# Where in its 256 bytes a stationary operand starts: AT_G from 56 to 16 elements

## The chip, the core and the metric

The kernel runs on one core of a Trainium2 chip. The metric is device time in microseconds (us), the median of several executions. The engines are TensorE (PE in the profile; its loads of stationary operands are listed as PEld), VectorE (DVE), ScalarE (ACT), GpSimd (POOL) and SyncE (SP), whose queue issues the transfers.

## What is computed

An attention over packed tokens feeds a two-layer network with silu. All arrays are float32.

```
p_packed = softmax(p k^T / 8) v             # 8 batches x 8 heads, 32 packed tokens from 576
x        = softmax(q p_packed^T / 8) p_packed   # then heads side by side: 4608 rows x 512
h        = x @ w_in                          # 512 -> 2048
g        = h * sigmoid(h)
out      = g @ w_out                         # 2048 -> 512
```

## The kernel before

Every large product is made of three products of halves. An operand is split into an upper part (a copy rounded to float32r, names that end in `_hi`) and a lower part (the operand less that copy, names that end in `_lo`), and upper by upper, upper by lower and lower by upper are added up in PSUM. In `nc.tensor.matmul(out, a, b)` the operand `a` is the stationary one: a weight load (LDWEIGHTS) puts its 128 columns into TensorE, and then the columns of `b` stream past.

The order of the work is written out by hand in `ORDER`, a text of steps, each a letter and a unit number, and the engines take the steps in that order. The first two batches run while the weights are still being made (up to about 195 us). After that come batches 2 to 7. A **pair unit** (there are 96: six batches, two halves of the rows, eight pairs of hidden blocks) covers 256 rows and two blocks of 128 hidden columns, and its output product is done with Strassen's scheme in seven products instead of eight. Its steps are

- `B`: `h_products` (L590), 12 matmuls with 288 moving columns; its stationary operands are `pw_hi` and `pw_lo`.
- `G` and `N`: `pair_values` (L612) and `rest_values` (L616), the silu on ScalarE. L612 writes the first four blocks of the tile `g`, eight blocks of 128 columns.
- `I`: `pair_sums` (L622 to L624) on GpSimd, four more blocks of `g` as sums and differences.
- `F`: `all_upper` (L638) on ScalarE, the upper part of seven of these blocks, 896 columns, into a tile `g_hi`.
- `L`: `all_lower` (L642) on VectorE, the lower part, into `g_lo`.
- `O`: `pair_products` with `terms` (L648), seven terms of three matmuls. The stationary operand is a block of 128 columns of `g_hi` or `g_lo`; the moving one is 256 columns of `wo_hi`, `wo_lo` or of `sums_of_w`, loaded from DRAM.

The tiles `g_hi` and `g_lo` come from the pool `gp_main`, two of each. They are 7 x 128 + 64 = 960 columns wide, so that the 896 columns of a pair unit may start anywhere in the first 64: `all_upper` starts them at `AT_G`. A row of a tile is 3840 bytes, 15 times 256, and in the built program every one of these tiles starts at a multiple of 256 bytes, as do the tiles of `wo_hi`, `wo_lo`, `sums_of_w`, `pw_hi`, `pw_lo` and `rest`. A block of 128 columns is 512 bytes, so all seven blocks of a unit start equally far past a multiple of 256.

A **rest unit** (16 of them: four for batches 0 and 1 together, twelve for batches 2 to 7) is the same for the 32 rows of each half that the pairs leave: 512 columns of `g_hi` and `g_lo` that start at 0, twelve matmuls of 512 moving columns, on the same lines L638, L642 and L648. The output product of the first two batches (also on L648, with `g_hi` and `g_lo` made at L602 and L608) has 512 moving columns and starts at 0 too.

Of the kernel before, what the change touches and what calls it, by code (L numbers as in the profile page):

```python
# [121 lines left out]

TP_BUFS = 4
EDGE = 504
AT_G = 56
ON_TOKENS = (0,)
SCALE = 1.0 / math.sqrt(D)
EPS = 1e-9
# [5 lines left out]
def packed_attention_ffn(ctx: ExitStack, tc: tile.TileContext, pkT, qT, v, w_in, w_out, out):  # L134
# [491 lines left out]
    def all_of(u):  # L626
        b, f, *more = units[u]
        if more:
            return rest[:, f : f + FJ].rearrange("p f e h s -> p (f e h s)")
        return hidden[u][:, P:]  # L630

    def all_upper(u):
        g = all_of(u)
        at = AT_G if g.shape[1] > FJ * P else 0
        both = [gp_main.tile([P, 7 * P + 64], F32R, name=name) for name in ("g_hi", "g_lo")]
# [284 lines left out]
```

## Time and profile before

| | |
|---|---|
| median of 3 executions | 694.07 us (693.35 to 694.8) |
| the profiled execution's own time | 693.81 us |
| its span | 692.0 us, granted TensorE clock 0.995 |
| busy: PE, PEld, DVE, ACT, POOL | 672.5, 591.5, 425.8, 387.0, 233.6 us |
| share of the chain that ended last: PE, DVE, ACT, DMA | 76%, 10%, 5%, 3% |

The span runs from the first to the last instruction that the profiler recorded; the profiled execution's own time holds 1.8 us outside it. Busy time counts the time in which at least one instruction of an engine was under way. A matmul's recorded duration holds its run through the array, so that matmuls in a row overlap; the distance of their starts, not the duration, says how fast they follow each other.

### The profile page before, as it was taken

Reading aid. Unit: us, or ns where it says so; the run is one execution under the profiler, and the core shown is the slowest. Engines: PE = TensorE matmul, PEld = TensorE weight load, DVE = VectorE, ACT = ScalarE, POOL = GpSimd, SP = SyncE. Lnnn points to the kernel's source line nnn. Section 1 sums busy time; section 2 is a strip of 40 time slices with the busy share of each in tenths; the row PEclk is TensorE's granted clock in tenths of the full one; section 3 lists DMA queues with packets and bytes.
Section 4 is the critical chain, followed back from the end, with each engine's and each line's share of the span. In section 5 each row is a group of like instructions: output and inputs, shape, how many; then the busy total and the mean of one; then the engine's idle time right before and its main releaser. Section 6 shows DMA issues by size and latency. Waiting matters only on the chain.

```text
span 692.0 us, 14725 instructions
## 1 busy us (share of the span) xinstructions
PE 672.5 (97%) x5958; PEld 591.5 (85%) x5958; DVE 425.8 (62%) x588; ACT 387.0 (56%) x641; POOL 233.6 (34%) x336
## 2 busy tenths in 40 slices
PE   7799999999999999999999999999999999999997
PEld 5477776788878998999888998899888898899995
DVE  5989989896774536753666425853665535663333
ACT  5787887463645535663556634755554754664431
POOL 1102054343203432544423343353251353435520
PEclk9899999999999999999999999999999999999999
DMA  9848864685967678967797578874994848685531
GB/s 362 328 136 307 282 222 173 235 267 184 386 242 283 247 245 329 363 251 262 283 342 282 184 284 308 348 279 131 353 353 168 303 132 307 265 313 190 212 139 45
DMA packets 55107, 178.62 MB, mean 258 GB/s; under 512 B 21760, under 2 KB 25856, under 8 KB 47360
## 3 DMA queue, kind: packets, MB, share of 16 engines
q1 hardware_dynamic: 54944, 177.56, 69.1%
q8 instruction: 47, 0.77, 0.4%
q10 hardware_dynamic: 96, 0.13, 0.1%
q14 instruction: 20, 0.16, 0.1%
HBM read 149.42 MB, written 24.12 MB: 251 GB/s over the span
## 4 chain that ended last, share of the span: by engine, by line
PE 76%; DVE 10%; ACT 5%; DMA 3%; issue 2%; POOL 2%; SPq 1%; ACTq 0%; DVEq 0%
PE ps_acc L648 45%; PE ps_two L590 23%; PE ps_two L287 5%; DMA win<-in_w_out 2%; PE ps_two L387 2%; DVE tm L423 1%; DVE g_lo L642 1%; DMA sums_of_w<-sums_of_w 1%; DVE g_lo L608 1%; DVE w_raw L252 1%; ACT g_hi L638 1%; DVE w_raw L256 1%; ACT g L612 1%; DVE wo_lo L280 1%; POOL g L623 1%
## 5 line engine op out<-in xcount | busy, mean ns | idle before, releaser
L642 DVE TENSOR_TENSOR g_lo<-g,g_hi 128x896 fp32r<-128x896 f32 x96 | 105.9, 1110 | 131.6 <-ACT g_hi L638 131.2
L648 PE MATMUL ps_acc<-wo_hi,g_hi 128*128 128x256 f32 (+1 forms) x576 | 184.7, 321 | 0.7 <-DVE o L790 0.7
L648 PE MATMUL ps_acc<-wo_hi,g_lo 128*128 128x256 f32 (+1 forms) x576 | 183.0, 318 | 2.2 <-DVE g_lo L608 2.2
L648 PE MATMUL ps_acc<-wo_lo,g_hi 128*128 128x256 f32 (+1 forms) x576 | 182.7, 317 | 0.0
L590 PE MATMUL ps_two<-a_hi,pw_hi 128*128 128x288 f32 x512 | 153.0, 299 | 1.5 <-DVE tm L423 1.5
L622 POOL TENSOR_TENSOR g<-g 128x128 f32<-128x128 f32 x96 | 56.2, 586 | 288.0 <-ACT g L612 287.9
L590 PE MATMUL ps_two<-a_lo,pw_hi 128*128 128x288 f32 x512 | 151.3, 295 | 0.0
L590 PE MATMUL ps_two<-a_hi,pw_lo 128*128 128x288 f32 x512 | 151.1, 295 | 0.0
L638 ACT CAST g_hi<-g 128x896 fp32r<-128x896 f32 x96 | 89.9, 942 | 77.6 <-POOL g L624 47.5
L648 PEld LDWEIGHTS ps_acc<-wo_hi,g_hi 128*128 128x128 f32 x576 | 108.1, 188 | 16.1 <-issue 5.6
L648 PEld LDWEIGHTS ps_acc<-wo_hi,g_lo 128*128 128x128 f32 x576 | 108.2, 188 | 12.4 <-DVE g_lo L608 4.7
L648 PE MATMUL ps_acc<-sums_of_w,g_hi 128*128 128x256 f32 x576 | 116.6, 284 | 0.0
L648 PEld LDWEIGHTS ps_acc<-wo_lo,g_hi 128*128 128x128 f32 x576 | 108.3, 188 | 6.8 <-DVE wo_lo L280 0.3
L590 PEld LDWEIGHTS ps_two<-a_hi,pw_hi 128*128 128x128 f32 x512 | 96.5, 188 | 14.4 <-PE ps_two L287 6.7
L590 PEld LDWEIGHTS ps_two<-a_lo,pw_hi 128*128 128x128 f32 x512 | 96.4, 188 | 0.8
L590 PEld LDWEIGHTS ps_two<-a_hi,pw_lo 128*128 128x128 f32 x512 | 96.5, 188 | 0.0
L648 PEld LDWEIGHTS ps_acc<-sums_of_w,g_hi 128*128 128x128 f32 x576 | 88.3, 188 | 8.9 <-issue 7.8
L648 PE MATMUL ps_acc<-sums_of_w,g_lo 128*128 128x256 f32 x288 | 80.5, 280 | 0.1
L623 POOL TENSOR_TENSOR g<-g 128x256 f32<-128x256 f32 x96 | 75.5, 787 | 6.6
L612 ACT ACTIVATE g<-ps_two 128x512 f32<-128x512 f32 x96 | 57.0, 598 | 33.4 <-DVE g_lo L642 16.8
L624 POOL TENSOR_TENSOR g<-g 128x128 f32<-128x128 f32 x96 | 53.2, 556 | 6.6
L648 PEld LDWEIGHTS ps_acc<-sums_of_w,g_lo 128*128 128x128 f32 x288 | 54.1, 188 | 0.4 <-DVE g_lo L642 0.3
(129 smaller groups left out, 799.7 us busy)
## 6 DMA issues: line engine op xcount, KB each, us to landing
sums_of_w<-sums_of_w SPq DMA_DIRECT2D x96, 768.0 KB, 6.2
w_quarter<-w_in SPq DMA_DIRECT2D x22, 1024.0 KB, 6.9
kvq_t<-in_v SPq DMA_DIRECT2D x8, 1280.0 KB, 8.8
kvq_t<-in_pkT SPq DMA_DIRECT2D x7, 1216.0 KB, 10.7
out<-o SPq DMA_DIRECT2D x16, 512.0 KB, 3.2
kvq_t<-in_qT SPq DMA_DIRECT2D x7, 1152.0 KB, 8.3
w_raw<-in_w_in SPq DMA_DIRECT2D x6, 1024.0 KB, 6.1
sums_of_w<-w_sums SPq DMA_DIRECT2D x8, 768.0 KB, 3.7
```

The costliest lines, as they stand in the source:

```text
L252: nc.vector.tensor_scalar(up.bitcast(F32), up.bitcast(F32), TOP, -TOP, op0=ALU.min, op1=ALU.max)
L256: nc.vector.scalar_tensor_tensor(low, up, -(2**31), low, op0=ALU.bitwise_and, op1=ALU.bitwise_or)
L287: nc.tensor.matmul(bank(par)[NP * i : NP * i + NP], lhs(r, i), rhs(r, i), start=True, stop=True)
L387: nc.tensor.matmul(self.ps[NP * i : NP * i + NP, par * D : par * D + D], e, vs[:n, c, h * D : h * D + D], start=(c == 0), stop=(c == 4),)
L590: nc.tensor.matmul(bank, p[:, par, cols], a[:, par], start=(n == 0), stop=(n == len(todo) - 1))
L612: nc.scalar.activation(g[:, : 4 * P].rearrange("p (e s) -> p e s", e=2), made["h", u, None][..., :MAIN], AF.Silu)
L622: nc.gpsimd.tensor_tensor(x[:, 4], x[:, 0], x[:, 2], ALU.subtract)
L623: nc.gpsimd.tensor_tensor(x[:, 5:7], x[:, 0:5:4], one, ALU.subtract)
L624: nc.gpsimd.tensor_tensor(x[:, 7], x[:, 3], x[:, 6], ALU.add)
L638: nc.scalar.copy(both[0], g)
L642: nc.vector.tensor_tensor(g_lo, g, g_hi.bitcast(F32), ALU.subtract)
L648: nc.tensor.matmul(out, g[:, rows], w, start=(first and n == 0), stop=(last and n == 2), skip_group_check=True)
```

## The change

`AT_G` is a number of float32 columns. At 56 the 896 columns of a pair unit's `g_hi` and `g_lo` start 224 bytes into their tiles, at 16 they start 64 bytes in. Nothing else differs: the tiles are as large and lie where they lay, and on every engine the same instructions stand in the same order.

```diff
--- before.py
+++ after.py
@@ -122,7 +122,7 @@
 
 TP_BUFS = 4
 EDGE = 504
-AT_G = 56
+AT_G = 16
 ON_TOKENS = (0,)
 SCALE = 1.0 / math.sqrt(D)
 EPS = 1e-9
```

## Rows read from the trace of the kernel before

**Rows 1.** Busy time of each engine by stretch; (x) counts instructions; PEclk is the granted clock.

```profile
core 0: us, PE busy (x) PEld busy (x) DVE busy (x) ACT busy (x) POOL busy (x), PEclk, DMA share, GB/s
...
215.00:370.00 155.00, 154.32 (x1487) 142.02 (x1486) 87.60 (x122) 83.93 (x138) 60.21 (x95) 1.00 0.77 284
370.00:520.00 150.00, 149.18 (x1448) 136.03 (x1447) 84.14 (x112) 83.29 (x135) 59.15 (x95) 1.00 0.75 281
520.00:676.00 156.00, 155.51 (x1349) 146.61 (x1348) 75.13 (x100) 79.46 (x133) 61.77 (x96) 1.00 0.61 224
```

**Rows 2.** Chain that ended last, 215 to 676 us, share by engine and line.

```profile
by line: PE ps_acc L648 51.2%; PE ps_two L590 28.3%; PE ps_two L287 5.3%; PE ps_two L387 1.8%; DVE tm L423 1.5%; issue 1.5%; DVE g_lo L642 1.4%; DMA sums_of_w<-sums_of_w 1.3%; ACT g_hi L638 1.0%; ACT g L612 0.9%; POOL g L623 0.8%; POOL g L6
```

**Rows 3.** Chain, 290 to 352 us, in order of time: start us, us, what.

```profile
298.32 0.95 ACT g_hi L638
299.29 1.18 DVE g_lo L642
...
311.51 0.95 ACT g_hi L638
...
340.65 2.01 DVE g_lo L642 x2
...
348.60 1.10 DVE g_lo L642
```

**Rows 4.** What TensorE itself waited for, 195 to 676 us: total us, times, longest.

```profile
PE ps_two L590 <- DVE tm L423: 1.2, 5, 0.2
PE ps_two L287 <- DVE tm L423: 0.5, 2, 0.2
```

**Rows 5.** Instructions on tiles `g_hi`: count, ns min/median/max, first and last start.

```profile
L648 PEld LDWEIGHTS ps_acc<-wo_lo,g_hi x576: 186/188/192, 38.1 to 687.2; 128*128 128x128 f32 x192
...
L648 PEld LDWEIGHTS ps_acc<-sums_of_w,g_hi x576: 186/188/192, 220.3 to 675.2; 128*128 128x128 f32 x192
...
L638 ACT CAST g_hi<-g x96: 925/943/968, 215.0 to 671.2; 128x896 fp32r<-128x896 f32 x96
L642 DVE TENSOR_TENSOR g_lo<-g,g_hi x96: 1027/1092/1465, 216.0 to 672.2; 128x896 fp32r<-128x896 f32 x96
...
L638 ACT CAST g_hi<-rest x16: 602/622/631, 196.3 to 682.4; 128x512 fp32r<-128x512 f32 x16
L642 DVE TENSOR_TENSOR g_lo<-rest,g_hi x16: 628/692/1233, 199.8 to 683.1; 128x512 fp32r<-128x512 f32 x16
```

**Rows 6.** All groups of instructions, shapes apart: L739 and L743, the sums of the weights.

```profile
L743 DVE TENSOR_TENSOR w_sums<-w_pair,w_sums 128x1024 fp32r<-128x1024 f32 x8 | 9.8, 1219 | 4.8 <-ACT w_sums L739 4.8
...
L739 ACT CAST w_sums<-w_pair 128x1024 fp32r<-128x1024 f32 x8 | 8.4, 1055 | 10.4 <-POOL w_pair L734 7.8 <-DMA first_sums<-w_sums 2.5
```

**Rows 7.** All groups of instructions, shapes apart: matmuls of L648 by operands and moving columns.

```profile
L648 PE MATMUL ps_acc<-sums_of_w,g_hi 128*128 128x256 f32 x576 | 116.6, 284 | 0.0
...
L648 PE MATMUL ps_acc<-wo_hi,g_hi 128*128 128x256 f32 x384 | 107.7, 281 | 0.0
L648 PE MATMUL ps_acc<-wo_lo,g_hi 128*128 128x256 f32 x384 | 107.5, 280 | 0.0
L648 PE MATMUL ps_acc<-wo_hi,g_lo 128*128 128x256 f32 x384 | 107.2, 279 | 0.0
...
L648 PE MATMUL ps_acc<-sums_of_w,g_lo 128*128 128x256 f32 x288 | 80.5, 280 | 0.1
```

**Rows 8.** Chain, 360 to 412 us, columns as in rows 3.

```profile
362.98 3.19 PE ps_two L590 x24
366.17 8.22 PE ps_acc L648 x36
...
382.40 3.20 PE ps_two L590 x24
385.60 4.95 PE ps_acc L648 x42
...
399.02 4.96 PE ps_acc L648 x42
```

**Rows 9.** Chain, 518 to 542 us, same columns.

```profile
520.77 4.96 PE ps_acc L648 x42
...
532.88 8.17 PE ps_acc L648 x36
```

## The prediction

> **What bounds the kernel now.** I read the time by stretches first. From 215 to 676 us, where all 96 pair units run, TensorE is busy in 154.32 + 149.18 + 155.51 = 459.0 of 461 us at a granted clock of 1.00, the full 2.4 GHz, while no other engine is busy much over half of the time [rows 1]. Then the chain of that stretch: its pieces on TensorE come to 51.2 + 28.3 + 5.3 + 1.8 = 86.6%, half of it on L648 alone, the line that reads the moved operands [rows 2]. The rest is short runs of ScalarE, VectorE and GpSimd such as [rows 3], in which the chain goes through the making of `g_hi` and `g_lo`. TensorE's own waits say how much slack is behind them: 1.7 us in all [rows 4]. So in this stretch time is the number of matmuls times the distance of their starts, and little could swallow a longer distance.
>
> **The change part by part.** No instruction is added, removed or moved, no transfer changes. What changes is the start address of three kinds of operation, by 224 - 64 = 160 bytes: the write of L638 on ScalarE, the second input and the output of L642 on VectorE, and the weight load of every matmul of a pair unit. I price each.
>
> *ScalarE and VectorE.* The same two lines run with operands at start 0 (the rest units, 512 columns) and at 224 (the pair units, 896). L638 takes 622 and 943 ns, L642 692 and 1092 ns [rows 5]. Both lines have a like at start 0 with 1024 columns, in the sums of the weights: L739 takes 1055 ns and L743 1219 ns [rows 6]. Between 512 and 1024 columns, all at start 0, ScalarE then needs (1055 - 622) / 512 = 0.846 ns a column and VectorE (1219 - 692) / 512 = 1.029, which gives 947 and 1087 ns for 896 columns; at 224 they are 943 and 1092. I see no sign of an address cost on these engines and put 0 for both. The bounds: 20 ns either way on each of 96 units of either line is 1.9 us of an engine's time, and it would count only where the chain runs through them, 1.0% and 1.4% of the stretch [rows 2], so under 0.1 us. TensorE's other work is the cover.
>
> *TensorE.* The pair units have 576 + 3 x 384 + 288 = 2016 matmuls of 256 moving columns [rows 7], 96 x 21. How closely do they follow each other? The chain lists unbroken runs: 42 of them take 4.95 or 4.96 us, 117.9 ns each [rows 8, 9]. With the stationary operand at start 0 the trace has two other lengths: 288 columns, 24 in 3.19 or 3.20 us, 133.1 ns each [rows 8], and 512 columns, 36 in 8.17 to 8.22 us, 226.9 to 228.3 ns [rows 8, 9]. A straight line through these two has (226.9 - 133.1) / 224 = 0.419 ns a column, and gives 133.1 - 32 x 0.419 = 119.7 ns for 256 columns (119.5 with 228.3). The pair units run at 117.9, some 1.6 to 1.8 ns less. So either the fixed part of a matmul is not the same for each length, or a stationary operand that starts 224 bytes in is changed over faster than one that starts at 0. The weight load's own record is no help: 186 to 192 ns in groups with both starts [rows 5].
>
> Counted against 256 columns at 2.4 GHz, 106.7 ns, the pair units pay 11.2 ns beside the columns; 288 columns (120.0 ns) pay 13.1 and 512 (213.3 ns) pay 13.6. By this the start at 0 is dearer by 1.9 to 2.4 ns.
>
> No row shows a start of 64. The ends are then: nothing (64 is as good as 224), and the dearest reading of a start at 0, 2.4 ns x 2016 = 4.8 us. Of the two starts that the trace shows, 64 is nearer to 0 than to 224, by 64 against 96 bytes when one goes round at 256. I take a straight line from 0 to 224, so that 64 keeps 160/224 = 0.71 of the penalty of 0: 0.71 x 1.6 ns = 1.14 ns, and times 2016 it is 2.3 us. On the path counts between the chain's 0.87 and all of it, 2.0 to 2.3 us; I take 2.1. The profiled execution, 693.81 us, becomes 695.9; the median of the runs shown is 0.26 us above it, so the forecast is 694.07 + 2.1 = **696.2 us**.
>
> *A rule against it.* The rows show a difference that fits the start address but could come from the number of columns [rows 8, 9]. The Trainium skill, TensorE: Matmul & The Clock Gate, section Part 2: What happens when you issue a matmul, says that TensorE reads the streaming and the stationary operand through two independent SBUF ports, so that loading the next weights takes nothing from the running matmul; and SBUF — State Buffer, section Specifications (TRN2), gives lines of 16 bytes, of which both 224 and 64 are multiples. By these the start makes no difference and the sum is 694.1 us. No run here shows which holds.
>
> **The rivals.**
> - *It does nothing that a clock can see (same).* The 1.6 ns belong to the number of columns and not to the start, or 64 is as far from trouble as 224 is. For it: the two lengths at start 0 do not lie on one line with 2.4 GHz exactly either (13.1 and 13.6 ns), so half a nanosecond depends on length anyway; ScalarE and VectorE show nothing. Time: 694.1, within 0.2%, which is about what a measurement of this kernel can tell from no change, 1.4 us or 0.7 ns a matmul.
> - *The full penalty of start 0 (slower, more).* If the changeover knows only "at or near the beginning of 256 bytes" and "near its end", 64 counts as the beginning. Time: 1.6 to 2.4 ns x 2016 = 3.2 to 4.8 us, so 697.3 to 698.9.
> - *64 is better than 224 (faster).* The fixed part is still 11.2 ns, so there is something left to win; if what matters is how far the stationary reads lag behind or lead the moving ones, which all begin at a multiple of 256, a lead of 64 may miss them better than 224, which is 32 short of the next multiple. It decides from 0.7 ns a matmul on; as large as the difference of 0 and 224 it would give 694.1 - 3.2 = 690.9. Nothing in the rows speaks for it beyond that the direction is unknown.
> - *VectorE's subtraction suffers.* L642 reaches 1465 ns in one of its 96 [rows 5]; were every one so slow, 96 x 0.37 = 36 us of VectorE, a little of it on the chain (1.4% x a third = 2 us, 696). But the starts on record agree, and I give it no chance of its own.
>
> **How the numbers follow.** Forecast (a part of the penalty, over 0.7 ns a matmul): 0.39. Full penalty: 0.12. Nothing: 0.37. Better: 0.12. So slower by over 0.2%: 0.51; within: 0.37; faster: 0.12. The forecast and the case of nothing are close; the differing fixed parts of a matmul tip it. The range for 8 in 10 leaves out most of the faster case and the dearest tail: from 693.0 (the case of nothing, with the scatter of the runs shown below it) to 699.0 (the full penalty by its dearest count). The forecast's own range is 695.5 to 697.3.
>
> **What would show it.** Right: in the chain after, unbroken runs of 42 matmuls on L648 take 4.98 to 5.03 us in place of 4.95 (118.6 to 119.7 ns each), while 24 of L590 stay at 3.2 us and 36 of the rest units at 8.2 us; L638 and L642 keep 943 and 1092 ns; and the span grows by about 2016 times the growth of that distance. Same: the 42 stay at 4.95 or 4.96. Wrong in the other direction: 4.92 or less. Wrong in kind: the 42 stay, and yet the span moves, with VectorE's or ScalarE's median moved, or with new waits of TensorE; or the 42 grow and the span doesn't, so that slack I did not see took it up.

## The result and the profile after

The changed kernel takes 687.55 us (median of 4 executions, 687.07 to 688.15) against 694.04 for the kernel before (4 executions); the ratio is 0.9907 with a 95% interval of 0.989 to 0.9924. It is faster by 6.5 us, where 2.1 us slower was forecast. The profiled execution took 688.15 us, its span is 686.4 us (692.0 before) at a granted clock of 0.994.

The stages of the changed kernel, columns as in [rows 1], the last one 5 us shorter since the pair units end earlier:

```profile
215.00:370.00 155.00, 153.93 (x1494) 141.24 (x1493) 89.13 (x124) 83.53 (x139) 61.44 (x96) 1.00 0.78 288
370.00:520.00 150.00, 149.03 (x1468) 136.16 (x1467) 84.53 (x115) 83.79 (x136) 58.12 (x93) 1.00 0.74 277
520.00:671.00 151.00, 149.91 (x1322) 140.97 (x1320) 73.36 (x97) 79.44 (x132) 61.45 (x96) 1.00 0.62 231
```

TensorE is as busy as before at the same clock; it gets through the same matmuls sooner. Where, the chain of the changed kernel shows (355 to 412 us, start us, us, what; the view of [rows 8]):

```profile
356.28 4.96 PE ps_acc L648 x42
361.24 3.19 PE ps_two L590 x24
364.44 8.19 PE ps_acc L648 x36
...
375.23 5.42 PE ps_acc L648 x33
380.65 3.19 PE ps_two L590 x24
383.84 4.78 PE ps_acc L648 x42
388.62 1.02 PE ps_two L287 x16
389.64 1.79 PE ps_two L590 x12
391.43 2.48 PE ps_acc L648 x21
393.91 3.19 PE ps_two L590 x24
397.10 4.78 PE ps_acc L648 x42
```

The reader is to see two things. L590 (24 in 3.19 us) and the rest unit's 36 matmuls of 512 columns (8.19 us) are as before. Of the pair units, the runs of 42 at 383.84 and 397.10 us, both behind L590, take 4.78 us, 113.8 ns a matmul, where runs of 42 behind L590 took 4.95 or 4.96 before [rows 8, 9]; but the 21 at 391.43 us still take 2.48 us, 118.1 ns each. (The 42 at 356.28 us begin behind other work; both its units run at 113.3 once they have begun.) So there are two spacings, not one smaller one. TensorE's own lines show them, first a fast unit, then a slow one (the changed kernel's timeline, start us, us, engine, line; a row with x2 holds two matmuls):

```profile
386.08 0.39 PE L648 MATMUL ps_acc<-sums_of_w,g_hi 128*128 128x256 f32 x2
386.31 0.28 PE L648 MATMUL ps_acc<-sums_of_w,g_lo 128*128 128x256 f32 x1
386.42 0.28 PE L648 MATMUL ps_acc<-wo_hi,g_hi 128*128 128x256 f32 x1
386.53 0.28 PE L648 MATMUL ps_acc<-wo_lo,g_hi 128*128 128x256 f32 x1
386.65 0.28 PE L648 MATMUL ps_acc<-wo_hi,g_lo 128*128 128x256 f32 x1
386.76 0.28 PE L648 MATMUL ps_acc<-wo_hi,g_hi 128*128 128x256 f32 x1
```

```profile
391.27 0.40 PE L648 MATMUL ps_acc<-sums_of_w,g_hi 128*128 128x256 f32 x2
391.51 0.28 PE L648 MATMUL ps_acc<-sums_of_w,g_lo 128*128 128x256 f32 x1
391.62 0.28 PE L648 MATMUL ps_acc<-wo_hi,g_hi 128*128 128x256 f32 x1
391.74 0.28 PE L648 MATMUL ps_acc<-wo_lo,g_hi 128*128 128x256 f32 x1
391.86 0.28 PE L648 MATMUL ps_acc<-wo_hi,g_lo 128*128 128x256 f32 x1
391.98 0.28 PE L648 MATMUL ps_acc<-wo_hi,g_hi 128*128 128x256 f32 x1
```

From the first row's start to the last one's are six matmuls: 0.68 us in the fast unit, 0.71 in the slow one (all the starts of the two units in the trace lie 113 to 114 and 117 to 119 ns apart). Taken from the starts of all matmuls in the trace, unit by unit and without gaps over 150 ns, the mean spacing over the 96 units is 117.8 ns before and 114.6 after. Before, every unit lies between 116.6 and 118.1; after, 17 units lie at 117.6 to 117.9 and the other 79 at 113.3 to 114.8 (distances of 113 and 114 ns, with a few longer ones where a unit begins). 3.1 ns x 2016 is 6.3 us, the change of the medians is 6.5.

ScalarE and VectorE did not move (instructions on `g_hi` in the changed kernel, the view of [rows 5]):

```profile
L638 ACT CAST g_hi<-g x96: 923/942/967, 214.8 to 665.8; 128x896 fp32r<-128x896 f32 x96
L642 DVE TENSOR_TENSOR g_lo<-g,g_hi x96: 1028/1092/1445, 215.7 to 666.8; 128x896 fp32r<-128x896 f32 x96
```

### The profile page after: what moved, and what is told of

It is laid out like the page before. It is cut to its first block, busy times and chain, and to the rows that moved or that the text cites. A ratio compares the mean times of both kernels' runs of the same rounds, so it can differ in the third digit from the quotient of the medians.

```text
span 686.4 us, 14725 instructions
## 1 busy us (share of the span) xinstructions
PE 666.2 (97%) x5958; PEld 585.7 (85%) x5958; DVE 425.3 (62%) x588; ACT 386.7 (56%) x641; POOL 233.7 (34%) x336
## 4 chain that ended last, share of the span: by engine, by line
PE 76%; DVE 11%; ACT 5%; DMA 3%; issue 2%; POOL 2%; SPq 1%; ACTq 0%; DVEq 0%
PE ps_acc L648 45%; PE ps_two L590 23%; PE ps_two L287 5%; DMA win<-in_w_out 2%; PE ps_two L387 2%; DVE tm L423 1%; DVE g_lo L642 1%; DMA sums_of_w<-sums_of_w 1%; DVE g_lo L608 1%; DVE w_raw L252 1%; ACT g_hi L638 1%; DVE w_raw L256 1%; DVE pw_lo L556 1%; ACT g L612 1%; DVE wo_lo L280 1%
## 5 line engine op out<-in xcount | busy, mean ns | idle before, releaser
L642 DVE TENSOR_TENSOR g_lo<-g,g_hi 128x896 fp32r<-128x896 f32 x96 | 106.0, 1112 | 129.5 <-ACT g_hi L638 129.2
L648 PE MATMUL ps_acc<-wo_hi,g_hi 128*128 128x256 f32 (+1 forms) x576 | 183.4, 318 | 0.8 <-DVE o L790 0.8
L648 PE MATMUL ps_acc<-wo_hi,g_lo 128*128 128x256 f32 (+1 forms) x576 | 182.0, 316 | 2.1 <-DVE g_lo L608 2.1
L648 PE MATMUL ps_acc<-wo_lo,g_hi 128*128 128x256 f32 (+1 forms) x576 | 181.5, 315 | 0.0
L590 PE MATMUL ps_two<-a_hi,pw_hi 128*128 128x288 f32 x512 | 153.4, 300 | 1.8 <-DVE tm L423 1.5
L590 PE MATMUL ps_two<-a_lo,pw_hi 128*128 128x288 f32 x512 | 151.3, 296 | 0.0
L590 PE MATMUL ps_two<-a_hi,pw_lo 128*128 128x288 f32 x512 | 151.3, 296 | 0.0
L638 ACT CAST g_hi<-g 128x896 fp32r<-128x896 f32 x96 | 89.8, 941 | 76.3 <-POOL g L624 44.7
L648 PEld LDWEIGHTS ps_acc<-wo_hi,g_hi 128*128 128x128 f32 x576 | 108.2, 188 | 15.9 <-issue 5.6
L648 PEld LDWEIGHTS ps_acc<-wo_hi,g_lo 128*128 128x128 f32 x576 | 108.3, 188 | 11.9 <-DVE g_lo L608 4.2
L648 PE MATMUL ps_acc<-sums_of_w,g_hi 128*128 128x256 f32 x576 | 114.9, 281 | 0.0
L648 PEld LDWEIGHTS ps_acc<-wo_lo,g_hi 128*128 128x128 f32 x576 | 108.2, 188 | 6.8 <-DVE wo_lo L280 0.3
L590 PEld LDWEIGHTS ps_two<-a_hi,pw_hi 128*128 128x128 f32 x512 | 96.5, 188 | 14.7 <-PE ps_two L287 6.7
L590 PEld LDWEIGHTS ps_two<-a_lo,pw_hi 128*128 128x128 f32 x512 | 96.5, 188 | 0.7
L590 PEld LDWEIGHTS ps_two<-a_hi,pw_lo 128*128 128x128 f32 x512 | 96.5, 188 | 0.0
L648 PEld LDWEIGHTS ps_acc<-sums_of_w,g_hi 128*128 128x128 f32 x576 | 87.8, 188 | 8.9 <-issue 7.8
L648 PE MATMUL ps_acc<-sums_of_w,g_lo 128*128 128x256 f32 x288 | 80.5, 280 | 0.2 <-DVE g_lo L642 0.2
L648 PEld LDWEIGHTS ps_acc<-sums_of_w,g_lo 128*128 128x128 f32 x288 | 54.1, 188 | 0.7 <-DVE g_lo L642 0.6
```

Of the source, the lines that this page charges most:

```text
L590: nc.tensor.matmul(bank, p[:, par, cols], a[:, par], start=(n == 0), stop=(n == len(todo) - 1))
L638: nc.scalar.copy(both[0], g)
L642: nc.vector.tensor_tensor(g_lo, g, g_hi.bitcast(F32), ALU.subtract)
L648: nc.tensor.matmul(out, g[:, rows], w, start=(first and n == 0), stop=(last and n == 2), skip_group_check=True)
```

## The experiments

**Other starts.** Theory one, "place": the weight load and the moving columns of the matmul before it read at places in 256 bytes, and some differences of their starts suit each other better. Rivals: "grid", a start at a multiple of 64 bytes is fast by itself, and the straight line of the prediction. Four starts, one execution each; each edit is one number in the kernel before (694.04 us; 692.94 in its one execution beside these four). The kernel before alone went from 692.54 to 694.80 us in its executions, so a single time tells little between two starts that differ by 1 us; the spacing tells more:

```diff
-AT_G = 56
+AT_G = 0      # start_0; 8: start_32, 32: start_128, 48: start_192
```

> AT_G 0, the pairs' parts start at a multiple of 256 bytes, as the moving operands do. Place theory (the weight loads and the moving columns are in each other's way when they start at the same place in 256 bytes, and 64 is clear of it): 42 matmuls take 4.95 to 5.03 us, 118 to 120 ns each, time 694 to 698 us. Grid theory (a start at a multiple of 64 bytes is fast, one between is slow): as at 64, 113 to 115 ns, 687.5 us. The prediction's own line from 0 to 224 gives 119.5 ns and 697 us.

> AT_G 8, a start of 32 bytes. Place theory: between 0 and 64, so 113 to 118 ns and 687 to 694 us, no sharper. Grid theory: slow as 224 is, 118 ns, 694 us.

> AT_G 32, a start of 128 bytes. Place theory: as far from 0 as it can be, so at least as fast as 64: 113 to 114.6 ns, 685 to 687.5 us. Grid theory: as at 64, 687.5 us. The prediction's line: 118.5 ns, 695 us.

> AT_G 48, a start of 192 bytes, 64 short of the next multiple of 256. Place theory, with place counted round the 256: near 224, so slow, 116 to 118 ns and 691 to 694 us; if only the distance to the moving operand's start counted it would be like 64, 687.5. Grid theory: as at 64, 687.5 us.

| start, bytes | time us | 42 in the chain near 385 us | mean ns a matmul, 96 units |
|---|---|---|---|
| 0 | 696.51 | 5.03 | 119.7 |
| 32 | 693.50 | 4.97 | 118.1 |
| 128 | 694.71 | 4.98 | 118.6 |
| 192 | 693.51 | 4.95 | 117.7 |

The chain of the kernel with start 0:

```profile
382.74 3.19 PE ps_two L590 x24
385.93 5.03 PE ps_acc L648 x42
```

Grid falls: 0, 128 and 192 are multiples of 64 and slow. The prediction's line is met at its end at 0 (119.5 to 119.7 ns for 256 columns) and at 128 (118.5), is 0.4 ns too high at 192 and 1.2 at 32, and misses 64 by 4.4. Place missed 128 by 4 ns. At 192 two units of 96 ran at 113.3 and 113.4 ns, the others at 117.7 to 118.3: the fast spacing exists there too, and is seldom entered. At 0 the 96 units settle: from the tenth matmul of a unit on, nearly every distance is 120 ns.

At the granted clock of 1.00, which is 2.4 GHz, 113.3 ns are 272 clock periods and 120 ns are 288: 16 and 32 more than one for each of the 256 columns. The spacing in between is no one number (in the kernel before, 116 to 120 ns from matmul to matmul). No run shows what sets these steps.

**Stationary start or difference.** Here every large tile is moved by 64 bytes, the moving operands with the stationary ones, so that the stationary start and its difference to the moving one come apart. One execution each; start_96 and pw_by_64 ran beside them (the kernel before: 693.68).

```diff
-    ident = const.tile([P, P + 352], F32, name="ident")
+    ident = const.tile([P, P + 368], F32, name="ident")
-EDGE = 504
-AT_G = 56
+EDGE = 488
+AT_G = 0      # all_by_64_start_0; 16: all_by_64_start_64
```

> Every large tile, stationary and moving, lies 64 bytes further, and the pairs' parts start at 0 in their tiles: the weight loads begin at 64, the moving operands too. Difference theory (what counts is the stationary start less the moving start): as start_0, 119.7 ns, 696.5 us. Address theory (the stationary start alone counts): as 64, 114.6 ns for the pairs, and L590's 288-column matmuls, whose stationary operand then begins at 64 too, faster than 133 ns: 686 us or less.

> Every large tile lies 64 bytes further and AT_G is 16: the weight loads of the pairs begin at 128, the moving operands at 64. Difference theory: as the changed kernel, 114.6 ns a matmul, 687.5 us. Address theory: as start_128 for the pairs, 118.6 ns.

Measured: 696.74 us with 119.7 ns, and 687.70 us with 114.8 ns. The first row is the chain of all_by_64_start_0, the second that of all_by_64_start_64:

```profile
386.26 5.03 PE ps_acc L648 x42
```

```profile
383.10 4.78 PE ps_acc L648 x42
```

Matmuls whose stationary operand begins at 64 are slow when the moving columns begin at 64 too; those whose stationary operand begins at 128 are fast when they begin at 64 (76 units of 96). It is the difference that counts, and address alone is out. Whether it is the difference to the moving columns of the same matmul or to those of the one ahead isn't shown, since all moving operands were moved together. In the first of the two L638 and L642 also work at 64, so they aren't what made the changed kernel faster.

> AT_G 24, a start of 96 bytes. If the place counts round 128 bytes (192 fell into the fast state in 2 of 96 units, 64 in most), 96 is as 224 is: 117.9 ns a matmul, 694 us. If 64 is the edge of a broad good region up to 128: 113 to 115 ns, 687 us.

693.68 us and 117.6 ns (42 in 4.93 us): 96 does as 224 does, and 64 is no edge of a broad good region. Of a place that counts round 128 bytes it says little, since most starts do as 224 does; against it stands that 192 was fast in 2 units and 64 in 79.

**How narrow.** Two theories on the fast spacing, a band or a smooth curve, and four starts round 64, one execution each (the kernel before: 694.10):

```diff
-AT_G = 56
+AT_G = 12     # start_48; 14: start_56, 18: start_72, 20: start_80
```

> AT_G 12, a start of 48 bytes. Two-spacings theory (at a difference of 64 a run of matmuls can lock into a spacing of 113.3 ns or into one of 117.8, and holds it until the run ends): if the fast spacing exists in a band round 64, some units at 113.3, the mean between 113.3 and 117.8, 686 to 694 us; if only at 64, all units at 118 and 694 us. Smooth-curve theory (the spacing falls evenly from 32 to 64): 116.3 ns in all units, 691 us.

> AT_G 14, a start of 56 bytes. Two-spacings theory with a band: as 64 or better, 113.3 ns in most units, 685 to 688 us; without: 118 ns, 694 us. Smooth-curve theory: 115.5 ns, 689 us.

> AT_G 18, a start of 72 bytes. Two-spacings theory with a band: as 64, which units are fast may differ, 685 to 690 us; without: 118 ns, 694 us. Smooth-curve theory (from 64 up to 96): 115.4 ns, 689 us.

> AT_G 20, a start of 80 bytes. Two-spacings theory with a band: some units at 113.3, 686 to 694 us; without: 118 ns, 694 us. Smooth-curve theory: 116.1 ns, 691 us.

| start, bytes | time us | 42 in the chain | mean ns, 96 units |
|---|---|---|---|
| 48 | 693.83 | 4.94 | 117.9 |
| 56 | 693.15 | 4.94 | 117.7 |
| 64 (changed kernel) | 687.55 | 4.78 | 114.6 |
| 72 | 693.94 | 4.97 | 118.4 |
| 80 | 695.38 | 4.99 | 118.7 |

The same stretch of the chain at 56 and at 72:

```profile
385.12 4.94 PE ps_acc L648 x42
```

```profile
385.22 4.97 PE ps_acc L648 x42
```

No unit of these four runs is at 113, the lowest is at 117.4; the nearest neighbours tried, 8 bytes off, have nothing of it. Band and curve both fall, the fast spacing belongs to 64 (and by two units to 192) among the starts tried.

**What puts a unit into one spacing or the other.** The matmuls ahead of a unit, L590's, were changed: their stationary operands `pw_hi` and `pw_lo` begin 64 or 192 bytes in, their moving ones stay. Lines of these two kernels are 3 higher, L590 is L593 and L648 is L651.

```diff
 # AT_G = 16; n, m = 16, 48: pw_by_64; 48, 16: pw_by_192
+    pad = lambda n: ent(tc.tile_pool(name=f"pad{n}", bufs=1)).tile([P, n], F32, name="pad")
+    pad(n)
     pw = ent(tc.tile_pool(name="pw", bufs=2))
+    pad(m)
...
+        pad(n)
         pw_b = ent(tc.tile_pool(name="pw_b", bufs=2, reuse_waits="tile"))
+        pad(m)
```

> The changed kernel, and the tiles pw_hi and pw_lo, the stationary operands of L590, also begin 64 bytes past a multiple of 256 (pads before and behind them); their moving operands a_hi and a_lo stay at 0 and 128. If the start matters for every matmul of this kind, the 1536 matmuls of L590 go from 133 ns to 127 to 130 ns: 4.6 to 9 us off 687.5, so 678.5 to 683 us. If it matters only where 256 columns hide the weight load barely: 133 ns still, 687.5 us.

> As pw_by_64, but pw_hi and pw_lo begin 192 bytes past a multiple of 256. If the state of a unit is handed over by the matmuls before it: other units slow than in the changed kernel, either more (as pw_by_64, 690 us) or fewer (down to 113.3 ns in all: 115 ns to 113.3 is 1.3 x 2016 = 2.7 us, 685 us). If it is not: the same 17 units slow, 687.5 us. L590 itself gains up to 1 ns a matmul, 1.5 us.

pw_by_64 took 689.62 us (one execution), and 56 units of 96 were slow; pw_by_192 took 688.51 us (4 executions; 0.9931 of the kernel before, 95% interval 0.9913 to 0.9949), with 27 slow. L590 itself hardly gained, 24 in 3.17 us in place of 3.19, so the 127 to 130 ns of the first case did not come. The chain of pw_by_64:

```profile
380.47 3.17 PE ps_two L593 x24
383.64 4.95 PE ps_acc L651 x42
388.58 1.02 PE ps_two L290 x16
389.60 1.79 PE ps_two L593 x12
391.39 2.39 PE ps_acc L651 x21
393.78 3.17 PE ps_two L593 x24
396.95 4.95 PE ps_acc L651 x42
```

Beside the changed kernel's chain this stretch is the mirror image: the units behind 24 matmuls of L593, fast there (4.78), are slow here (4.95), and the 21 behind a run of L593 that follows L290, slow there (2.48), are fast here (2.39). Over the whole trace the first half of this is the rule: of the 20 units that come behind 24 matmuls of L590 with another unit ahead of those, 1 is slow in the changed kernel, 19 in pw_by_64 and 12 in pw_by_192. The second is not: of the 9 behind 12 matmuls of L590 that follow L287, 3 are slow in the changed kernel, 3 in pw_by_64 and none in pw_by_192. So the matmuls ahead have a part in the spacing that a unit takes, and the unit keeps it: 26 units follow another unit without a break, and in the changed kernel and in these two each of them has the spacing of the one ahead.

> The changed kernel once more, beside these: 687.5 us. If the state of a unit is set by what runs before it, which is the same in every execution: about the same 17 of 96 units are slow. If it falls by chance: another set.

688.06 us (4 executions; 0.9922 of the kernel before, 0.9906 to 0.9939). 17 units slow again, and 13 of them the same ones. The spacing of a unit is mostly the same from one execution to the next; the few that fell the other way (four slow ones in each) come from something that differs between executions, which isn't shown.

**Within a unit.** Only the tiles at the right end are moved by 64 bytes, so that in each unit the 9 matmuls with `sums_of_w` have a difference of 0 and the 12 with `wo_hi` and `wo_lo` one of 64. (The `g_hi` and `g_lo` of the first two batches lie at that end as well and move to 64, and with them the 384 matmuls of 512 columns that read them.)

```diff
-EDGE = 504
-AT_G = 56
+EDGE = 488
+AT_G = 16
```

> The changed kernel with the tiles at the right end, sums_of_w and w_quarter among them, 64 bytes further: 9 of the 21 matmuls of a unit (moving operand sums_of_w) have a difference of 0, the other 12 (wo_hi, wo_lo) keep 64. If the spacing is set matmul by matmul: 9 at 119.7 and 12 at 113.3, mean 116, 691 us. If a run locks as a whole and a difference of 0 breaks the lock: no unit under 117, 694 to 696 us.

692.33 us in one execution (the kernel before: 693.38), a mean of 116.9 ns with units from 116.2 to 118.3. The chain:

```profile
385.19 4.89 PE ps_acc L648 x42
```

Neither number fits cleanly: no unit locks into 113.3, as the second theory has it, but the mean lies nearer to the first. The starts in the trace say more. From the tenth matmul of a unit on, each place in the unit has a distance of its own, the same within 1 ns in over nine of ten units: 119 and 113 ns between the three matmuls with `sums_of_w`, then 117, 122, 116 and 114. Before that, at the end of the only six matmuls in a row with a difference of 64, it comes down to 113 or 114 in most units. So the spacing is set matmul by matmul, by those just ahead as well, and not by one value for each difference. The time holds one thing more: in the first two batches the matmuls of 512 columns go from 229 to 233 ns, some 1.5 us for all 384 by estimate; the next experiment meets this again.

**512 columns.** The rest units, which begin at 0, are moved to 64 as well:

```diff
 # AT_G = 16
-        at = AT_G if g.shape[1] > FJ * P else 0
+        at = AT_G
```

> The changed kernel with the rest units' g_hi and g_lo at 64 too, 192 matmuls of 512 moving columns. If the start counts for every length by as much as for 256 columns: 192 x 5 ns = 1 us off, 686.5 us; if only where the weight load fills nearly the whole matmul: 227 ns still, and at most the unit behind a rest unit changes state: 687.5 us, within 0.3.

688.83 us (4 executions; 0.9934 of the kernel before, 0.9919 to 0.9948; the changed kernel beside it 0.9922, 0.9906 to 0.9939). The chains of rest_by_64 and of the changed kernel's second run, the same rest units:

```profile
363.82 8.39 PE ps_acc L648 x36
...
529.08 8.39 PE ps_acc L648 x36
```

```profile
363.80 8.21 PE ps_acc L648 x36
...
528.87 8.17 PE ps_acc L648 x36
```

Neither theory holds: with 512 moving columns a difference of 64 is slower, 233 ns a matmul against 227 to 228. The times of the two kernels can't be told apart, the matmuls can. No version tried beats the changed kernel.

## Why the prediction was wrong

- **What bounds the kernel**: right. TensorE's spacing alone moved the time: 3.1 ns x 2016 = 6.3 us of the 6.5, and nothing took any of it up; its own waits in the stage stay small, 2.5 us against 1.7 [rows 4].
- **ScalarE and VectorE at 0**: right, 942 against 943 ns and 1092 against 1092 [rows 5].
- **The start at 0**: right, though drawn from matmuls of other lengths. 119.7 ns (119.5 by the other reading) was read off the line through 288 and 512 columns, and start_0 measured 119.7 (696.51 us, 3.6 more than the kernel before beside it; 1.9 ns x 2016 = 3.8). So start 224 really was better than 0. That the weight load's record is no help holds for the trace it was said of: L590's loads, which begin at 0, take 188 ns there like those of the pair units at 224.
- **The step that failed** is "I take a straight line from 0 to 224, so that 64 keeps 160/224 = 0.71 of the penalty of 0". It put 64 at 1.1 ns a matmul above 224, and 64 measured 3.1 ns below. Between 0 and 224 the spacing is no line: 119.7, 118.1, 117.9, 117.7, **114.6**, 118.4, 118.7, 117.6, 118.6, 117.7 and 117.8 ns at 0, 32, 48, 56, 64, 72, 80, 96, 128, 192 and 224. All starts but one lie within 2.1 ns; 64 stands apart, 3 to 4 ns below its neighbours, and there 79 of 96 units hold a second, faster spacing.
- **The rival "64 is better than 224"** was the case, and one half of the reason that it gave is borne out by the pair of kernels with all tiles moved: what counts is the stationary start against the moving one. The other half, that a lead of 64 is farther from trouble than 224, is not: 96 and 128 are farther still, and slow. Nothing in the rows of the kernel before singled out 64. Its chance of 0.12 was too low and its price too small: 3.2 us, the distance of 0 and 224, where 6.5 was measured. The range ended at 693.0, with the lower bound of the change taken as nothing although no row excluded a gain.
- **The rule against it**: the Trainium skill, TensorE: Matmul & The Clock Gate, section Part 2: What happens when you issue a matmul, has the weight load and the moving operand on two independent ports. What the prediction drew from that, a start that makes no difference, is not what the runs show: with the same instructions, the spacing moves between 113.3 and 119.7 ns with the difference of the two start addresses. No run shows whether the ports are where it comes from.

Open: what in the hardware makes 64 the place, and why 512 columns answer the other way. The runs show that the difference of the starts decides which spacings a run of matmuls can hold, and that the matmuls ahead have a part in which one it takes; no run shows the reads themselves.

## What to carry to other kernels

Where TensorE does nothing but matmuls of few moving columns, each with a weight load of its own, the start of the stationary operand against the moving one is a free parameter worth a sweep in small steps: here 8 bytes decided 0.8% of the time. A line between two measured starts said nothing of the one between them, and a bound should then be kept open on both sides. Judge by the spacing of the matmuls in unbroken runs, which came out alike within 0.2 ns in runs with the same differences (114.6, 114.7 and 114.8; 119.7 and 119.7), and for each length apart.

## What was not expected of the hardware

- At a difference of 64 a run of matmuls of 256 columns holds one of two spacings, 113.3 or 117.8 ns, to the end of its unit and into the next one (17 of 96 units slow in the changed kernel, 17 again in a second run, 56 and 27 with other matmuls ahead).
- The fast spacing was found at a difference of 64 bytes, in 2 units of 96 at 192, and in none at 56 or 72 or at the other starts tried.
- At a difference of 64, 512 columns take 233 ns against 227 to 228 at 0 in the rest units, and 233 against 229 in the first two batches: the better start depends on the length.
